# Computing an SSM convolution kernel only at its 641 distinct bf16 positions, and expanding it by DMA

## The chip, the cores and the metric

One core of a Trainium2 chip. The metric is the device time of one execution in microseconds (us), the median of several runs; "span" is the profiled time of the core from its first to its last instruction, about 2 us less. PE is TensorE, DVE VectorE, ACT ScalarE, POOL GpSimd; SP (SyncE) mainly issues DMAs. A run counts as slow when it is over 1.5% above the fastest of its kernel.

## The reference, cut to what matters

```python
def _B_ref(u, A_re, A_im, B_re, B_im, C_re, C_im, log_dt, Dskip):   # u: (1, 2048, 512); A, B, C: (512, 128)
    dt = jnp.exp(log_dt)[:, None]
    logdA = dt * (A_re + 1j * A_im)
    dB = dt * Bc
    l = jnp.arange(L).astype(A_re.dtype)          # bf16: 2048 positions, 641 distinct values
    P = jnp.exp(logdA[:, :, None] * l)            # (512, 128, 2048)
    K = jnp.einsum("dn,dnl,dn->dl", Cc, P, dB).real
    ...                                           # y = irfft(rfft(u) * rfft(K)) + u * Dskip
x = A_x
x = x + attention(layernorm(x)); x = x + _B_ref(layernorm(x))    # and both once more, same weights
```

The positions are rounded to bf16, so above 256 they come in steps of 2, 4 and 8, and several of the 2048 positions share one value of K. K does not depend on x; it is computed once, transformed (the "spectrum"), and used in both convolution layers.

## The kernel before

K at position i·32 + j is the sum over the 128 states of G[i]·Z[j]: two tables of complex powers, 64 by 33, built by repeated doubling on VectorE and contracted on TensorE, for nine chunks of channels. Every doubling is one complex multiply:

```python
def cmul(nc, pool, shape, xr, xi, c, s, out_r, out_i, nz, tag):
    # ... t1, t2 from a pool with one buffer each
    nc.vector.tensor_tensor(t1[:], xr, c, ALU.mult)
    nc.vector.tensor_tensor(t2[:], xi, s, ALU.mult)
    nc.vector.tensor_tensor(out_r, t1[:], t2[:], ALU.add if nz else ALU.subtract)
    # ... t3, t4: the same two buffers again
    nc.vector.tensor_tensor(t3[:], xi, c, ALU.mult)
    nc.vector.tensor_tensor(t4[:], xr, s, ALU.mult)
    nc.vector.tensor_tensor(out_i, t3[:], t4[:], ALU.subtract if nz else ALU.add)
```

The result, `kg_sb`, lies on 64 partitions in 33 KB each. The spectrum relays it to 128 partitions with two DMAs, permutes it into `k_perm` with two copies, and makes the rounding by 20 patch copies (15 on VectorE, 5 on ScalarE).

```python
with tc.tile_pool(name="kpool", bufs=1) as kpool:
    kg_sb = kpool.tile([NI, NJ, D], BF16, name="kg_sb")       # 33 KB, kept until the spectrum is done
    ...
    k_spectrum(tc, nc, kg_sb, C, w2_dram, kf_dram)            # k_perm, then a1s (two buffers), kf_sb (three)
x_sb = xpool.tile([P, NA, D], F32, name="x_sb")               # 32 KB
with tc.tile_pool(name="xin", bufs=1) as tmp:
    xin = tmp.tile([P, NA, D], BF16, name="xin")              # 16 KB
    nc.sync.dma_start(xin[:], A_x...)
    # ... ScalarE: casts into x_sb and the layer-norm sums of its 16 rows
```

The order of instructions on each engine and the addresses of pools are decided by the framework: a scheduler orders, and a pool that is released gives its address to the next one.

## Time and profile before

| | us |
|---|---|
| median of the three runs at the start | 806.27 (802.87 to 843.03; the run of 843.03 was slow) |
| span of the profiled run | 804.0 |
| powers and tables (DVE full) | up to 229 |
| PE tail, relay, copies and patches | 229 to 264.1 |
| spectrum, x's casts and statistics | 264.1 to 326.1 |
| four layers | 326.1 to 804.0 |

The page cuts the span into 40 slices, a digit being the busy share in tenths. Two of its rows, kernel before:

```profile
DVE  7999998989742730358999968665457999968665
DMA  2010000000028263000300027633000300044732
```

This fence shows what an average hides: DVE is full in the first eleven slices (20 us each), then little used for five, then works in the layers. The prediction below shows the same stretches in microseconds.

### The profile page before, as it was taken

To read this page: it belongs to the slowest core of one execution; us is meant where nothing else is said; L and a number is where in the kernel's file an instruction comes from. 1 tells how busy PE (TensorE), PEld (TensorE's weight loads), DVE (VectorE), ACT (ScalarE), POOL (GpSimd) and SP (SyncE) were. 2 spreads that over 40 slices of the span, in tenths; PEclk is the share of its full clock that TensorE was granted. 3 is DMA by queue.
4 is the path that set the end of the run, shared out by engine and by line. 5 is a ranking of instruction groups with operands and counts; after the bars stand their busy time and mean duration, and the time that the engine had idled before them with its cause. 6 is when DMAs were issued, how large, how long until landed. Compare 5 with 4: busy or idle time off the path is not lost. (4 is left out here: it accounts for less than half of the span.)

```text
span 804.0 us, 14299 instructions
## 1 busy us (share of the span) xinstructions
PE 489.9 (61%) x5960; PEld 389.3 (48%) x5960; DVE 601.4 (75%) x1079; ACT 366.0 (46%) x596; POOL 14.6 (2%) x20
## 2 busy tenths in 40 slices
PE   1002877676930720499887767563599887858554
PEld 1002877676930720344655646553344655637553
DVE  7999998989742730358999968665457999968665
ACT  7960223232333669643242337536543243237524
POOL 0000000000000000100000010000100000010000
PEclk9999999999999955599898888787698998887878
DMA  2010000000028263000300027633000300044732
GB/s 46 26 52 0 1 28 27 26 27 27 2 42 278 99 228 94 0 1 2 92 2 1 2 104 233 191 106 104 2 1 1 93 2 2 1 179 155 200 101 104
DMA packets 23318, 53.87 MB, mean 67 GB/s; under 512 B 6203, under 2 KB 8408, under 8 KB 21208
## 3 DMA queue, kind: packets, MB, share of 16 engines
q1 hardware_dynamic: 20870, 49.23, 19.3%
q10 hardware_dynamic: 2304, 2.62, 0.9%
q0 software_dynamic: 80, 1.11, 0.5%
q8 instruction: 46, 0.75, 0.4%
q14 instruction: 18, 0.15, 0.1%
HBM read 36.57 MB, written 10.49 MB: 59 GB/s over the span
## 5 line engine op out<-in xcount | busy, mean ns | idle before, releaser
L813 PE MATMUL pk<-Zr,Gr 128*64 128x33 bf16 x512 | 118.5, 290 | 79.5 <-DVE Gr L672 78.8
L813 PEld LDWEIGHTS <-Gr 128*64 128x64 bf16 x512 | 107.0, 211 | 79.7 <-issue 63.1
L814 PE MATMUL pk<-Zn,Gi 128*64 128x33 bf16 x512 | 117.4, 287 | 25.8 <-DVE Gi L677 25.8
L814 PEld LDWEIGHTS <-Gi 128*64 128x64 bf16 x512 | 105.2, 207 | 27.6 <-DVE Gi L677 27.3
L263 PE MATMUL po<-ident,pav 128*128 128x128 bf16 x1024 | 75.2, 245 | 9.5 <-DVE pav L259 9.2
L263 PEld LDWEIGHTS <-pav 128*128 128x128 bf16 x1024 | 71.7, 113 | 12.5 <-DVE pav L259 12.3
L816 ACT CAST kg_sb<-pk 64x264 bf16<-64x264 f32 x64 | 23.8, 373 | 116.8 <-PE pk L814 116.8
L208 DVE TENSOR_TENSOR prod<-qT,kT_ext 128x2048 bf16<-128x2048 bf16 x64 | 75.1, 1215 | 1.6 <-ACT qT L187 1.6
L259 DVE TENSOR_TENSOR pav<-attn,v_ext 128x2048 bf16<-128x2048 bf16 x64 | 74.4, 1220 | 2.3 <-PE po L263 2.1
L547 PE MATMUL pb<-Wp,t 128*128 128x128 bf16 x256 | 37.7, 241 | 32.9 <-DVE t L535 29.4
L152 PE MATMUL pt<-ident,xn 128*128 128x128 bf16 x128 | 15.8, 278 | 55.9 <-ACT xn L124 54.1
L270 ACT CAST oT<-po 128x1024 bf16<-128x1024 f32 x8 | 8.1, 1012 | 85.2 <-PE po L263 85.2
L211 PEld LDWEIGHTS <-prod 128*128 128x128 bf16 x1024 | 31.1, 97 | 23.6 <-DVE prod L208 16.4
L547 PEld LDWEIGHTS <-t 128*128 128x128 bf16 x256 | 27.7, 109 | 30.2 <-DVE t L535 30.0
L211 PE MATMUL L<-ind,prod 128*128 128x8 bf16 x1024 | 33.8, 167 | 13.0 <-DVE prod L208 13.0
L152 PEld LDWEIGHTS <-xn 128*128 128x128 bf16 x128 | 11.4, 126 | 61.7 <-ACT xn L124 58.1
L534 ACT CAST ub<-pb 128x1024 bf16<-128x1024 f32 x32 | 32.3, 1031 | 19.7 <-DVE t L536 18.4
L500 PE MATMUL pb<-a1s,w_sb 128*128 128x64 bf16 x768 | 32.0, 201 | 15.1 <-DVE kf_sb L479 8.7
L500 PEld LDWEIGHTS <-w_sb 128*128 128x128 bf16 x768 | 28.6, 103 | 17.9 <-issue 15.1
L103 ACT ACTIVATE ln_junk<-x_sb 128x512 bf16<-128x512 f32 x48 | 30.2, 628 | 14.5 <-DVE x_sb L99 13.1
L548 PE MATMUL pb<-WpJ,t 128*128 128x128 bf16 x256 | 36.2, 240 | 0.1
L289 PE MATMUL pq<-wvp,xnT 128*128 128x512 bf16 x128 | 34.7, 414 | 1.0 <-DVE v_ext L294 1.0
(234 smaller groups left out, 1148.9 us busy)
## 6 DMA issues: line engine op xcount, KB each, us to landing
w_sb<-w_dram SPq DMA_DIRECT2D x12, 1024.0 KB, 9.1
kr_c<-kf_dram SPq DMA_DIRECT2D x64, 128.0 KB, 2.9
ki_c<-kf_dram SPq DMA_DIRECT2D x64, 128.0 KB, 2.9
kf_dram<-kf_sb SPq DMA_DIRECT2D x16, 256.0 KB, 3.0
v_ext<-v_ext SPq DMA_DIRECT2D x2, 1568.0 KB, 9.0
w_dram<-w_full SPq DMA_DIRECT2D x4, 512.0 KB, 2.6
w_dram<-w_full ACTq DMA_DIRECT2D x4, 512.0 KB, 2.6
xin<-in_A_x_dram SPq DMA_DIRECT2D x1, 2048.0 KB
```

Source lines behind the costliest of these rows:

```text
L103: nc.scalar.activation(lnst["junk"][:], x_sb[:, a, :], ACT.Square, accum_out=lnst["s2"][:, a:a + 1])
L208: eng.tensor_tensor(pr[:], qT[:, ft].unsqueeze(1).to_broadcast([P, NW, 4, P]), kap, ALU.mult)
L211: nc.tensor.matmul(L[:, al, w0 + wi, ft * 8:(ft + 1) * 8], lhsT=pr[:, wi, al, :], rhs=ind8[:], start=False, stop=True, skip_group_check=True)
L259: eng.tensor_tensor(pv[:], attn[:, :, w, :].unsqueeze(2).to_broadcast([P, 4, DH, H]), v[:, s0:s0 + 4, :].rearrange("p a (d h) -> p a d h", ...
L263: nc.tensor.matmul(po[:, al, ftp, :], lhsT=pv[:, al].rearrange("p d h -> p (d h)")[:, ftp * P:(ftp + 1) * P], rhs=ident[:], start=False, s ...
L289: nc.tensor.matmul(pp[:], lhsT=xnT[:, dt, a * P:(a + 1) * P], rhs=wv[:, dt].rearrange("p d h -> p (d h)"), start=(dt == 0), stop=(dt == ND ...
L500: nc.tensor.matmul(p2[:, j, :], lhsT=self.w2[:, ec * EC + j, :], rhs=a1s[:, ec * EC + j, :], start=True, stop=True)
L534: nc.scalar.copy(ub[:], p2[:].rearrange("p e q -> p q e"))
L547: nc.tensor.matmul(p3[:, j, :], lhsT=t1[:, dql, :], rhs=wp_r, start=True, stop=False)
L548: nc.tensor.matmul(p3[:, j, :], lhsT=t2[:, dql, :], rhs=wpj_r, start=False, stop=True)
L813: nc.tensor.matmul(pk[:, j, :], lhsT=Gr[:, :, dl], rhs=Zr[:, :, dl], start=True, stop=False)
L814: nc.tensor.matmul(pk[:, j, :], lhsT=Gi[:, :, dl], rhs=Zn[:, :, dl], start=False, stop=True)
```

## The change

Intent: compute K at the 641 distinct positions only. They form a rectangle of two tables, 32 powers (multiples of 8, table A) by 21 others (table B); for four groups of channels side by side that fills TensorE's 128 rows. The compact kernel goes to DRAM in 24 stores, and 18 loads expand it to the 2048 positions, repeating rows, so that the patches vanish.

```diff
-        chunks = [(c * DC, DC) for c in range(D // DC - 1)] + [(D - DC, DC // 2), (D - DC // 2, DC // 2)]
-        for dc, (d_lo, dcs) in enumerate(chunks):
-            ...            # two levels of table Z, three of table G, per chunk of 64 channels
+        for c in range(P // CH):                      # 4 chunks of 32 x 4 channels
+            Ar = tb.tile([P, CH, NIA, 4], BF16, name="A_r")
+            ...
+            for k in range(5):
+                J = 1 << k
+                shape = [P, CH, J, 4]
+                y = [t[:, k, qs, :].unsqueeze(2).to_broadcast(shape) for t in (Pr, Pi)]
+                cmul(nc, tmpp, shape, [t[:, :, 0:J, :] for t in (Ar, Ai)], y, [t[:, :, J:2 * J, :] for t in (Ar, Ai)])
+            for q8 in range(CH // 8):
+                ...        # 16 matmuls of 84 columns, one eviction into kgs
+        for g in range(4):
+            ...            # six pieces each
+            for dst, sr in pieces:
+                nc.sync.dma_start(dst, sr)            # 24 stores kgs -> kd_dram, 641 x 512
@@ k_spectrum
-            for jhi in range(2):
-                (nc.sync if jhi == 0 else nc.gpsimd).dma_start(kr0[jhi::2, :, :], kg_sb[:, 16 * jhi:16 * jhi + 17, :])
+            nc.sync.dma_start(dsk[:], ins["Dskip"].partition_broadcast(1))
+            k_load(tc, nc, kr, kd)                    # 18 loads kd_dram -> k_rl, 12 of them with repeated rows
+            nc.vector.tensor_tensor(kr[0:1, 0, :], kr[0:1, 0, :], dsk[:], ALU.add)
             ...            # the two permuting copies stay
-            for (p0, p1, runs) in round_patches():
-                ...        # 20 patch copies and the copy of the first 16 rows
@@ main
-    with tc.tile_pool(name="kpool", bufs=1) as kpool:
-        kg_sb = kpool.tile([NI, NJ, D], BF16, name="kg_sb")
+    kd = dram.tile([NROW, D], BF16, name="kd_dram")
```

## The prediction

> **What bounds the kernel now.** I read the busy tenths of the page first, then the busy time by stretches, then the timelines of VectorE (DVE) and of the DMA-issuing SyncE queue around the ends of those stretches. The page's slices show a first third unlike the rest: DVE full, TensorE (PE) clock full, hardly any DMA. Cut at the events of the timeline, the stretches are (us, then busy us and instruction counts by engine, clock, DMA share, GB/s):
>
> ```profile
> 0.00:15.30 15.30, 3.33 (x24) 2.23 (x24) 11.44 (x47) 11.02 (x23) 1.58 (x13) 1.00 0.26 61
> 15.30:54.70 39.40, 0.00 (x0) 0.00 (x0) 39.12 (x63) 36.03 (x71) 0.00 (x0) 1.00 0.07 27
> 54.70:229.00 174.30, 113.91 (x963) 112.14 (x963) 162.78 (x341) 51.90 (x106) 0.00 (x0) 1.00 0.05 19
> 229.00:236.90 7.90, 6.95 (x62) 6.83 (x62) 0.41 (x1) 1.84 (x5) 0.00 (x0) 1.00 0.00 0
> 236.90:253.20 16.30, 0.00 (x0) 0.00 (x0) 0.00 (x0) 0.02 (x1) 0.69 (x1) 1.00 0.94 251
> 253.20:264.10 10.90, 0.00 (x1) 0.03 (x1) 8.44 (x17) 8.62 (x6) 0.00 (x0) 1.00 0.51 213
> 264.10:326.00 61.90, 20.99 (x512) 19.30 (x512) 19.39 (x20) 49.14 (x85) 0.34 (x1) 0.67 0.42 137
> 326.00:804.00 478.00, 344.74 (x4400) 248.78 (x4400) 359.85 (x592) 207.45 (x305) 11.98 (x5) 0.84 0.23 70
> ```
>
> The columns after the length are PE, weight loads, DVE, ScalarE (ACT), POOL. Up to 54.7 the powers are squared and the first tables built, DVE full. From 54.7 to 229 nine chunks expand both tables by complex multiplies and contract them: DVE 93% busy, PE 114 us hidden under it. From 229 PE finishes alone, from 236.9 everyone waits for the DMA that relays the kernel onto 128 partitions, from 253.2 copies permute and patch it. At 264.1 the spectrum starts. So this whole front is serial and DVE sets 213.7 us of it (15.3 to 229). The rest of the program, 539.9 us, is not touched by the change.
>
> DVE timeline near the end of the tables, and the copies after the relay:
>
> ```profile
> 223.04 0.42 DVE L676 TENSOR_TENSOR c_b<-Gr,pow_i_hi 128x512 bf16<-128x512 bf16 x1
> 223.38 0.68 DVE L670 TENSOR_TENSOR c_a<-Gr,pow_r_hi 128x1024 bf16<-128x1024 bf16 x1
> 223.98 0.42 DVE L677 TENSOR_TENSOR Gi<-c_a,c_b 128x512 bf16<-128x512 bf16 x1
> 224.31 0.69 DVE L436 TENSOR_SCALAR g_i<-g_i 128x1024 int32<-128x1024 int32 x1
> 224.91 0.68 DVE L671 TENSOR_TENSOR c_b<-Gi,pow_i_hi 128x1024 bf16<-128x1024 bf16 x1
> 225.63 0.69 DVE L672 TENSOR_TENSOR Gr<-c_a,c_b 128x1024 bf16<-128x1024 bf16 x1
> 226.36 0.69 DVE L675 TENSOR_TENSOR c_a<-Gi,pow_r_hi 128x1024 bf16<-128x1024 bf16 x1
> 226.97 0.69 DVE L676 TENSOR_TENSOR c_b<-Gr,pow_i_hi 128x1024 bf16<-128x1024 bf16 x1
> ...
> 253.29 1.49 DVE L608 COPY k_perm<-k_rl 128x4096 bf16<-128x4096 bf16 x1 [16.49 <-DMA k_rl<-kg_sb]
> 256.83 1.76 DVE L619 COPY k_perm<-k_perm 32x512 bf16<-32x512 bf16 x7 [2.06 <-ACT k_perm L608]
> 258.62 2.36 DVE L622 COPY k_perm<-k_rl 16x8192 bf16<-16x8192 bf16 x1
> ```
>
> Two things to see. Start to start, a 512-element multiply takes 0.34 us, a 1024-element one 0.60 (and a 2048-element one 1.13, from 172.59 to 173.72): 0.067 us plus 1 us per 1920 elements. And where an operation needs the result just before it (224.91 to 225.63), or overwrites what that one reads (225.63 to 226.36), the step is 0.72 to 0.73, not 0.60: a dependence costs 0.12 us. The old order mostly has another instruction in between.
>
> **What the skill says.** "VectorE: DVE Perf Modes", "The perf-mode tier table": bf16 tensor_tensor from SBUF reaches 2x, 2048 elements in 1224 ns; the trace has 1216 to 1220. "Vector Engine (DVE) Microarchitecture Reference", "5.1 Performance modes": this mode asks for 2-byte types, innermost step of one and more than one element innermost, not for long rows. That matters, as the new tables have innermost runs of 4. No two-source instruction here has such short rows, but the 16x8192 copy into runs of 4 took 2.36 us, far above one element per cycle. "DMA: Bandwidth & Descriptors", "Anatomy of one DMA": a fixed cost near 2 us, mostly the write receipt; here the stores of the spectrum landed in 2.0 us at the least and 2.9 in the median. Its "Specifications" want 512 B for line rate and say that smaller transfers are read-modify-written; the new scatter writes 256 B rows, and no row of this trace is a store of that kind.
>
> **The change part by part.** The 2048 positions rounded to bf16 have 641 distinct values, in place of 64x33 computed ones.
>
> *Setup.* Twelve powers for eleven, so 11 squarings. The 21-entry table B takes 7 complex multiplies over 13 blocks of 512: 13x512 = 6,656 elements, times 6 instructions, the same 6,656 as the old first tables. 6x6,656/1920 = 20.8 us, plus 42x0.067 = 2.8: 23.6 us. Little is saved here.
>
> *Chunks.* Before, each of 512 channels got 80 new table entries: 80x512x6 = 245,760 elements, plus table copies. Now table A gets 31 entries in 4 chunks of 32x4 channels: 3,968x6x4 = 95,232 elements in 120 instructions: 49.6+8.0 = 57.6 us, against 174.3 wall.
>
> *DVE sum from 15.3* (where the first power is ready in both): squarings 20x0.60 = 12.0; B 23.6; A 57.6; the rest of the C.B product 2.4; sine constants and small ones, now all inside this phase, 10.6: 106.2 us. The built order of instructions runs each complex multiply as two products, a sum that needs them, and so on, in the same pair of temporaries: 4 dependences in 6. 20x4 for A and about half that rate for B, less the interleaved constants, gives some 85x0.12 = 10 us. The middle squarings have no table work beside them and are paced by ACT (four instructions of 0.52 us start to start per level): 4 us idle. Tables end at 15.3+106.2+10+4 = 136 (estimate), against 229.
>
> *PE.* 256 matmuls of 84 columns for 1,024 of 33 at 0.117 us each. They hide except in the last chunk: 64 matmuls; the first matmul pairs of the spectrum, 128 columns, were 0.105 us apart at half clock, so I take 0.085: 5.4 us, plus the last eviction (264 columns took 0.37, 1024 took 1.01, so about 0.7 for 672). End 142; this tail was 7.9 and is 6.
>
> *Relay.* Removed: the two DMAs (16.3 us, slowed by the 4 MB of the DFT table beside them) and 10.9 us of copies with patches. Added, all on the SyncE queue: 24 stores of the compact kernel to DRAM, then 18 loads with broadcast rows. They are issued one at a time, each also waiting for the eighth one before it. Issues here took 0.32 (128 rows), 0.59 (64 rows), 0.59 to 0.69 (32 rows), 0.84 to 0.90 us (odd shapes); I take 0.55. Ahead of them in the queue are the skip vector and a quarter of the DFT table: 1.5 us. So 1.5 + 24x0.55 (13.2) + landing 2.5 + 18x0.55 (9.9) + landing 2.6 = 29.7. Then the skip add 0.4 and the two permuting copies (ACT's took 3.6): 4.1. Spectrum start 142+29.7+4.1 = 176.
>
> *Sum.* 264.1-176 = 88 us: 93 from the tables, 2 from the tail, 7 given back (34 us of relay for 27). 804-88 = 716 us. What follows is taken as unchanged: the remaining 3 MB of the DFT table are issued behind the loads but needed only some 7 us after the spectrum starts.
>
> **The rivals.** (1) Runs of 4 lose the 2x mode. Then A costs 95,232/960+8 = 107 us and B 44: 70 us more, about 786. For: no two-source proof in the trace. Against: the rule looks at the innermost step alone, and the copies with the same runs kept their fast mode. About 6%. (2) DMA takes the place of DVE: 256 B stores or the chain of 42 issues cost twice what I take. Issues of 0.9 us would add 15 us, slow stores some 15 more: 730 to 745. For: every odd-shaped DMA here cost 0.8 to 0.9. Against: the 256 B loads at the start (512 rows each) landed in 2.3 to 3.8 us with issues of 0.37 to 0.50. (3) ACT becomes the bound, having all sine constants and 44 power copies in less time: its work from 47 to 76 is about 28 us, so it fits under DVE, but a late constant stalls DVE in order; up to 8 us. (4) Issues as cheap as 0.35 and no idle in setup: some 12 us better, 704.
>
> **Range and chances.** These sum to more room upwards than downwards: 716, range 700 to 742. A gain under 2% would need 788 us or more: mode loss together with a slow relay. The fast runs before were 802.9 and 806.3, so their spread hardly matters. Faster 0.97, within 2% 0.02, slower 0.01.
>
> **What would show it.** The 128x2048 multiply of table A at 1.22 us (2.29 would be rival 1); DVE over 90% busy from 15 to about 136; dependent steps 0.12 us longer; table phase 57.6 plus some 9 us for four chunks; PE under 2 us busy per group of 16 matmuls; stores and loads on the SyncE queue together near 30 us, and their single issue times; copies after it, then the spectrum start at about 176; from there to the end 540 us. The prediction is wrong if the relay runs past 45 us, if DVE shows idle time waiting for ACT constants over 10 us, or if the part after the spectrum start changes by more than 5 us, say because the late DFT table holds up its second stage.

## The result and the profile after

| | before | after |
|---|---|---|
| median of four runs, us | 804.57 (801.53 to 843.03) | 717.88 (716.43 to 718.44) |
| span of the profiled run | 804.0 | 715.9 |

The ratio is 0.892 (95% interval 0.888 to 0.896): 11% less time. A ratio is the mean time of one kernel's fast runs over that of the other's of the same rounds, so it is not quite the ratio of the medians. Predicted were 716 us, 700 to 742.

The same two rows of the page, kernel after (a slice is now 18 us):

```profile
DVE  7999999304500348899995867635689999858665
DMA  2002110237661000300002766040003000083622
```

DVE's full stretch is 7 slices instead of 11, and the gap behind it did not shrink. By stretches, kernel after (start:end, length, then busy us and instruction counts of PE, weight loads, DVE, ACT, POOL; PE's clock, DMA share, GB/s):

```profile
15.00:61.57 46.57, 0.00 (x0) 0.00 (x0) 45.88 (x86) 44.27 (x85) 0.00 (x0) 1.00 0.06 23
61.57:131.50 69.93, 12.95 (x194) 11.84 (x194) 67.21 (x130) 32.56 (x54) 0.00 (x0) 0.73 0.11 46
131.50:136.80 5.30, 3.85 (x62) 3.69 (x62) 0.51 (x1) 2.84 (x4) 0.00 (x0) 0.69 0.00 0
136.80:167.50 30.70, 0.00 (x0) 0.00 (x0) 0.41 (x1) 0.00 (x0) 0.00 (x0) 0.52 0.59 142
...
168.90:236.20 67.30, 19.69 (x512) 17.82 (x512) 18.91 (x17) 51.51 (x85) 0.35 (x1) 0.65 0.44 155
236.20:715.90 479.70, 341.71 (x4374) 251.15 (x4400) 359.63 (x596) 208.06 (x306) 11.96 (x5) 0.83 0.23 70
```

Both table stretches keep DVE over 96% busy, so DVE still sets their end. In the relay's 30.7 us no compute engine works. The stage from the spectrum start to the end of the statistics is 67.8 us (168.9 to 236.8; the stretch above is cut 0.6 us too early); its counterpart before was 62.0.

DVE's timeline at the end of the last table, kernel after:

```profile
127.13 1.23 DVE L629 TENSOR_TENSOR A_r<-cm_a,cm_b 128x2048 bf16<-128x2048 bf16 x1
128.39 1.22 DVE L631 TENSOR_TENSOR cm_a<-A_i,pow_r 128x2048 bf16<-128x2048 bf16 x1
129.53 1.22 DVE L632 TENSOR_TENSOR cm_b<-A_r,pow_i 128x2048 bf16<-128x2048 bf16 x1
130.78 1.22 DVE L633 TENSOR_TENSOR A_i<-cm_a,cm_b 128x2048 bf16<-128x2048 bf16 x1
```

1.22 us for 2048 elements although the innermost run is 4: the fast mode held. Start to start, the independent pair (128.39, 129.53) is 1.14 us apart, the dependent pair (129.53, 130.78) 1.25. The DMA issues of SyncE, kernel after (start, length, instruction, count):

```profile
136.80 14.83 SPq L780 DMA_DIRECT2D kd_dram<-kgs  x24
...
152.15 9.04 SPq L803 DMA_DIRECT2D k_rl<-kd_dram  x17
161.23 1.73 SPq L458 DMA_DIRECT2D w_sb<-w_dram  x3
178.38 14.70 SPq L599 DMA_DIRECT2D kf_dram<-kf_sb  x12
193.81 0.33 SPq L861 DMA_DIRECT2D xin<-in_A_x_dram  x1
```

and the last two kinds in the kernel before:

```profile
273.54 3.71 SPq L635 DMA_DIRECT2D kf_dram<-kf_sb  x4
277.42 0.33 SPq L876 DMA_DIRECT2D xin<-in_A_x_dram  x1
```

The relay takes 14.8 us of stores and 9.5 us of loads (the first of the 18 is not in the row above), near what was worked out, and then 6.3 us until the last load has landed. But look at the load of x: before, it was issued behind 4 stores of the spectrum, 13.3 us after the spectrum start (264.1); after, behind 12 of them, 24.9 us after its start (168.9). ACT's casts and statistics of x, some 31 us in series, wait for it and end the stage. That is the 6 us, and the question of the experiments is what delays x.

### The profile page after: what moved, and what is told of

Read it like the earlier page. It is cut to its first block, busy times and chain, and to the rows that moved or that the text cites. A ratio compares the mean times of both kernels' runs of the same rounds, so it can differ in the third digit from the quotient of the medians.

```text
span 715.9 us, 12534 instructions
## 1 busy us (share of the span) xinstructions
PE 381.7 (53%) x5166; PEld 286.6 (40%) x5192; DVE 504.4 (70%) x873; ACT 351.0 (49%) x552; POOL 13.8 (2%) x19
## 5 line engine op out<-in xcount | busy, mean ns | idle before, releaser
L259 PE MATMUL po<-ident,pav 128*128 128x128 bf16 x1024 | 77.4, 250 | 9.0 <-DVE pav L255 8.9
L259 PEld LDWEIGHTS <-pav 128*128 128x128 bf16 x1024 | 74.4, 115 | 11.6 <-DVE pav L255 11.4
L760 PE MATMUL pk<-B_r,A_r 128*128 128x84 bf16 x128 | 16.5, 251 | 95.6 <-DVE A_r L629 95.6
L760 PEld LDWEIGHTS <-A_r 128*128 128x128 bf16 x128 | 15.0, 130 | 96.2 <-ACT w_qi L398 66.8
L207 PE MATMUL L<-ind,prod 128*128 128x8 bf16 x1024 | 33.8, 167 | 13.2 <-DVE prod L204 13.1
L496 PE MATMUL pb<-a1s,w_sb 128*128 128x64 bf16 x768 | 31.0, 197 | 9.0 <-DVE kf_sb L475 3.3
L285 PE MATMUL pq<-wvp,xnT 128*128 128x512 bf16 x122 | 32.0, 391 | 2.0 <-DVE v_ext L290 1.5
L486 PE MATMUL pb<-F1c,u 128*64 128x128 bf16 x256 | 21.0, 251 | 21.6 <-issue 21.3
L275 PE MATMUL pq<-wop,oT 128*128 128x512 bf16 x120 | 28.9, 379 | 6.7 <-ACT oT L266 6.1
L473 ACT CAST z<-pb 128x1024 bf16<-128x1024 f32 x16 | 16.2, 1012 | 32.7 <-PE pb L544 32.5
L496 PEld LDWEIGHTS <-w_sb 128*128 128x128 bf16 x768 | 27.4, 100 | 12.1 <-issue 9.2
```

Source lines behind the costliest of these rows:

```text
L207: nc.tensor.matmul(L[:, al, w0 + wi, ft * 8:(ft + 1) * 8], lhsT=pr[:, wi, al, :], rhs=ind8[:], start=False, stop=True, skip_group_check=True)
L259: nc.tensor.matmul(po[:, al, ftp, :], lhsT=pv[:, al].rearrange("p d h -> p (d h)")[:, ftp * P:(ftp + 1) * P], rhs=ident[:], start=False, s ...
L275: nc.tensor.matmul(pw[:], lhsT=oT[:, al, ftp, :], rhs=wo[:, ftp, :], start=(ftp == 0), stop=(ftp == NDT - 1))
L285: nc.tensor.matmul(pp[:], lhsT=xnT[:, dt, a * P:(a + 1) * P], rhs=wv[:, dt].rearrange("p d h -> p (d h)"), start=(dt == 0), stop=(dt == ND ...
L496: nc.tensor.matmul(p2[:, j, :], lhsT=self.w2[:, ec * EC + j, :], rhs=a1s[:, ec * EC + j, :], start=True, stop=True)
L760: nc.tensor.matmul(o, lhsT=ta[:, ql].rearrange("p i g -> p (i g)"), rhs=tbb[:, c * CH + ql].rearrange("p b g -> p (b g)"), start=(kx == 0) ...
```

## The experiments

All outputs are right. Each edit is against the changed kernel unless it says otherwise; ratios are to the kernel before, where the change alone has 0.892. One hundredth of ratio is 8 us. The medians are over all timed executions; those of pad (one of 2002 us) and best_c (one of 678.79) include one slow execution, which the ratios leave out.

| run | median us | ratio | 95% |
|---|---|---|---|
| xin_pool | 724.28 | 0.898 | 0.895 to 0.901 |
| before_xin_pool | 809.77 | 1.005 | 1.001 to 1.009 |
| cmul_order | 708.26 | 0.878 | 0.875 to 0.881 |
| two_queues | 712.85 | 0.885 | 0.882 to 0.889 |
| pad | 715.35 | 0.886 | 0.883 to 0.889 |
| pad2 (same program) | 710.62 | 0.883 | 0.881 to 0.886 |
| before_pad | 811.81 | 1.007 | 1.004 to 1.009 |
| w2_early | 719.32 | 0.892 | 0.889 to 0.894 |
| x_early | 693.66 | 0.861 | 0.858 to 0.864 |
| big_first | 722.78 | 0.899 | 0.895 to 0.902 |
| best_b | 675.73 | 0.841 | 0.838 to 0.844 |
| best_c | 675.38 | 0.837 | 0.832 to 0.841 |

### What delays x: first theory, the queue (xin_pool, before_xin_pool)

```diff
-        nc.sync.dma_start(xin[:], A_x.rearrange("b (p a) d -> p (b a) d", p=P))
+        nc.gpsimd.dma_start(xin[:], A_x.rearrange("b (p a) d -> p (b a) d", p=P))
```

> The changed kernel with one word different: the load of x is issued by GpSimd's queue, not by SyncE's, where it stood behind 12 spectrum stores (before the change: behind 4). My theory of the 7.1 us that the part after the spectrum start lost: x is issued 24.9 us after that start instead of 13.3, and ScalarE's 31 us of casts and statistics, which end the stage, follow it. Then x is issued about 13 us after the start, the statistics end 59 to 62 us after it instead of 67.3, and the whole is 6 us shorter (3 to 10): ratio to the kernel before about 0.884 where the change alone had 0.892. The rival, that the late quarters of the DFT table or slow spectrum stores stretch the stage: x arrives sooner but the evictions and stores still end late, and the total stays within 2 us.

> The kernel before the change with the load of x on GpSimd's queue. There x was issued 13.3 us after the spectrum start, as soon as its buffer was free, so my theory expects little: within 2 us of the kernel before (0 to -2), and the part from the spectrum start to the end as long as in the changed kernel with the same edit, to 2 us. If instead both kernels gain alike, the queue's order is not what made the parts differ, and the 7 us have another cause (the clock, the late table).

The first miss: the changed kernel became 5 to 6 us slower, not faster. On its new queue, with nothing ahead of it, x was issued at 196.69, 26.9 us after the spectrum start. What POOL waited for, run xin_pool (engine, instruction, releaser: us, times, longest):

```profile
POOL xin L861 <- DVE kf_sb L475: 193.7, 1, 193.7
```

It waited for an eviction of the spectrum's second stage, which has nothing to do with x's data. That pointed to a wait for the buffer. So the twelve stores ahead of x in SyncE's queue were a symptom: the scheduler put x where its buffer comes free. (POOL's load landed 9.9 us after its issue.) The kernel before lost 3 to 4 us with the same edit (809.77 against 806.49), where at most a gain of 2 was expected; its issue, 14.2 us after the spectrum start, was hardly later than before. The second half of that expectation missed too: from the spectrum start to the end the two kernels with the same edit took 542.1 and 552.4 us, so they still differ by 10 us, and the queue is not what makes them differ.

### Second theory, the address (pad, pad2, before_pad)

The compiled programs' buffer maps (byte of the partition where each starts) say:

```
                     before             after
kg_sb   (33 KB)      29600              -
k_perm  (16 KB)      63392              29600
a1s, 1st and 2nd     79776, 96160       45984, 62368
x_sb    (32 KB)      29600              29600
xin     (16 KB)      62368              62368
```

Before, xin lay on the end of kg_sb and on k_perm, which is free when the first stage has read it. With kg_sb gone everything slid down, and xin lies exactly on the second a1s buffer, read until the last matmuls of the second stage. What SyncE waited for before it issued x's load (L861), run after:

```profile
SPq L861 <- PE pb L496: 0.6, 1, 0.6
```

L496 is the second stage's matmul: its last one ends at 193.78, and x is issued at 193.81. In the kernel before, x is issued at 277.42, 0.4 us after the last matmul that reads k_perm (277.05). If this is the cause, 33 KB of padding undo it, and padding in the kernel before brings it in:

```diff
+    padp = tc.alloc_tile_pool(name="padp", bufs=1)                # pad: where kpool was
+    padt = padp.tile([P, 33, D], BF16, name="padt")
+    nc.vector.memset(padt[:, 0, 0:1], 0.0)
     btmp = tc.alloc_tile_pool(name="ctmp_b", bufs=1)
     ...
     k_spectrum(tc, nc, kd, ins, C, w2_dram, kf_dram)
+    padp.release()
```

```diff
     with tc.tile_pool(name="xin", bufs=1) as tmp:                 # before_pad: in the kernel before
+        padt = tmp.tile([P, 33, D], BF16, name="padt")
+        nc.vector.memset(padt[:, 0, 0:1], 0.0)
         xin = tmp.tile([P, NA, D], BF16, name="xin")              # now at 96160, the second a1s
```

> The changed kernel with a 33 KB buffer, touched once and otherwise unused, where the kernel before kept its kernel table until the spectrum was done. New theory of the 7 us that the later part lost, after the queue swap made nothing faster: the change took that 33 KB buffer away, so the buffers above slid down, and x's landing buffer now lies at the address of the second first-stage buffer of the spectrum, which is read until the spectrum's last matmuls, where before it lay on the permuted kernel, free after the first stage. So x can't be fetched earlier, whatever queue issues it. With the pad the addresses are those of before: x is issued 13 to 15 us after the spectrum start, not 24.9, the statistics end 60 to 63 us after it, not 67.3, total 6 us less (3 to 9). Rival (the late quarters of the DFT table, or spectrum stores): within 2 us of the changed kernel.

> The reverse in the kernel before: its buffer for x alone is pushed up by 33 KB (an unused tile ahead of it in the same pool), onto the second first-stage buffer of the spectrum, as in the changed kernel. Theory of the addresses: x is issued some 25 us after the spectrum start instead of 13.3, the statistics end 65 to 69 us after it instead of 61.4, and the total is 6 us longer than the kernel before (3 to 9; ratio 1.004 to 1.011). Rival (what the change itself did to the table or the stores): no difference, ratio 0.998 to 1.002.

> The same program as the one labelled pad, run again because its only profiled execution took 2002 us (every engine several times slower than elsewhere) and shows no usable durations; its five timed ones gave 0.8862 of the kernel before. Theory of the addresses: in a normal profile x is issued behind 4 stores, 13 to 16 us after the spectrum start instead of 24.9, the statistics end 61 to 64 us after it instead of 67.3, total 711 to 716. If the statistics still end 67 us after it, the gain came from elsewhere and the theory falls.

The one profiled execution of pad took 2002 us, for no reason that I can name; its durations are not used. SyncE's issues in before_pad, then in pad2:

```profile
274.43 15.48 SPq L635 DMA_DIRECT2D kf_dram<-kf_sb  x12
290.74 0.33 SPq L878 DMA_DIRECT2D xin<-in_A_x_dram  x1
```

```profile
178.94 3.71 SPq L599 DMA_DIRECT2D kf_dram<-kf_sb  x4
182.77 0.36 SPq L865 DMA_DIRECT2D xin<-in_A_x_dram  x1
```

and pad2 by stretches from its spectrum start:

```profile
169.47:230.90 61.43, 21.06 (x512) 19.42 (x512) 18.91 (x17) 50.64 (x85) 0.35 (x1) 0.64 0.51 171
230.90:710.20 479.30, 344.82 (x4400) 247.80 (x4400) 360.11 (x596) 208.03 (x306) 11.95 (x5) 0.83 0.23 70
```

| | x issued after the spectrum start | statistics end after it | spectrum start to end |
|---|---|---|---|
| before | 13.3 | 62.0 | 539.9 |
| before_pad | 26.3 | 70.1 | 548.9 |
| after | 24.9 | 67.8 | 547.0 |
| pad2 | 13.3 | 62.1 | 540.7 |

The address alone moves the stage both ways, by 6 to 8 us and the whole later part by 6 to 9, and with the old addresses the later part of the changed kernel is as long as that of the kernel before, to 1 us. These are single profiled executions (before_pad's was its slowest); by the medians the totals move by 6 us (before_pad) and 7 us (pad2). The 4 and 12 stores ahead of x come and go with it, and x follows the last reader of its bytes each time: in before_pad the last second-stage matmul ends at 290.71 and x is issued at 290.74, in pad2 the last matmul on k_perm ends at 182.45 and x is issued at 182.77. This settles the cause. It also answers the prediction's own guess:

### The late DFT table (w2_early)

```diff
+    cb["w2"] = ...   # a buffer at the far end of memory; its four loads after chunk 3, not at the spectrum
```

> The changed kernel with the 4 MB DFT table fetched in four pieces during the last chunk of table A, into its own buffer at the far end of memory, where the DMA engines are idle, instead of around the relay. Theory: the last three quarters saturated the DMA engines beside the last loads of the relay (6.1 us to land, where a lone one took 2.1), and the first quarter took the queue's time ahead of the stores: the spectrum starts 3 us sooner (2 to 5), and that reaches the end: total 3 us less (1 to 5). Rival: the late table also held the part after the spectrum start; then the statistics end less than 65 us after that start and the total falls by 6 or more. Other rival: the loads land no sooner, the total stays within 1 us.

Neither the theory nor the first rival: ratio 0.892 as without the edit, the spectrum start at 169.29, the rest 548.1. The other rival is right, the loads land no sooner. The 6.1 us that the largest load takes do not come from the table (5.9 us with it away), and the late table did not hold the end. It did slow the first stores: beside its first quarter, issued just ahead, the first store landed 4.9 us after its issue, with the table away 2.0.

### Dependences (cmul_order)

```diff
-    t1, t2 = tmp("cm_a"), tmp("cm_b")
+    t1, t2, t3, t4 = tmp("cm_a"), tmp("cm_b"), tmp("cm_c"), tmp("cm_d")
     nc.vector.tensor_tensor(t1, xr, yr, ALU.mult)
     nc.vector.tensor_tensor(t2, xi, yi, ALU.mult)
-    nc.vector.tensor_tensor(out[0], t1, t2, ALU.subtract)
-    t3, t4 = tmp("cm_a"), tmp("cm_b")
     nc.vector.tensor_tensor(t3, xi, yr, ALU.mult)
     nc.vector.tensor_tensor(t4, xr, yi, ALU.mult)
+    nc.vector.tensor_tensor(out[0], t1, t2, ALU.subtract)
     nc.vector.tensor_tensor(out[1], t3, t4, ALU.add)
```

> The changed kernel with each complex multiply as four products into four temporaries, then the difference and the sum: the same six instructions, but only one in six now follows its own input directly. Theory (VectorE sets the end of the tables, and a dependence on the neighbour costs 0.12 us): some 70 to 85 dependences at 0.12 us, so the tables end 8 to 10 us sooner, at 122 to 124 instead of 132.0, and all of it reaches the end: 8 us (6 to 10) off the total. Rival (TensorE or ScalarE paces the chunks, or the dependence costs nothing): tables within 2 us of 132, total within 2 us.

DVE's timeline at the end of the last table, run cmul_order:

```profile
118.34 1.22 DVE L630 TENSOR_TENSOR cm_d<-A_r,pow_i 128x2048 bf16<-128x2048 bf16 x1
119.47 1.22 DVE L631 TENSOR_TENSOR A_r<-cm_a,cm_b 128x2048 bf16<-128x2048 bf16 x1
120.61 1.22 DVE L632 TENSOR_TENSOR A_i<-cm_c,cm_d 128x2048 bf16<-128x2048 bf16 x1
```

Same instructions, same 1.22 us each, but 1.13 to 1.14 us start to start, also between the last product and the difference that it does not feed. The tables end at 121.8 instead of 132.0, 10.2 us sooner, and the total falls by about as much (9.6 by the medians). Counted in the trace, 74 of the 161 steps that follow an instruction of these multiplies in the changed kernel come 0.11 to 0.19 us later than the prediction's formula for independent ones (0.067 us plus 1 us per 1920 elements), 9.3 us in all; in cmul_order none of 162 does. Theory confirmed: DVE sets that end. The prediction's 85 dependences of 0.12 us were some 10 too many, and their sum of 10 us was the right size.

### What bounds the relay (two_queues, big_first)

```diff
-                nc.sync.dma_start(dst, sr)
+                (nc.sync if n % 2 == 0 else nc.scalar).dma_start(dst, sr)     # and so for 17 loads
```

> The changed kernel with its 24 stores and 17 expanding loads of the relay issued in turn by SyncE's and ScalarE's queues instead of SyncE's alone. Theory (the relay is bound by issuing one after the other, 24 x 0.618 and 18 x 0.525 us): 14.8 us of stores become about 8 and 9.5 us of loads about 5, while landings and the table's DMA stay: relay 31.4 to 19 us (17 to 22), total 10 to 13 us less. Rival (the DMA engines are bound by the many short rows, or eight outstanding per queue holds them): the relay keeps over 28 us and the total moves by at most 3.

A miss: spectrum start at 164.6 instead of 168.9, 4 us and not 10 to 13. ACT issued its 12 stores in 8.65 us, SyncE needed 12.91 for its 12. What SyncE's queue waited for, run two_queues, and the stretch of the loads:

```profile
SPq L780 <- DMA kd_dram<-kgs: 5.0, 3, 4.6
SPq L803 <- DMA k_rl<-kd_dram: 4.5, 4, 3.0
```

```profile
149.80:163.00 13.20, 0.00 (x0) 0.00 (x0) 0.41 (x1) 0.03 (x1) 0.00 (x0) 0.50 0.99 181
```

With one queue the waits were 0.3 (stores, for a load of the table) and 1.0 (loads). The program lets a DMA start only when an earlier one, eight places back, has landed; issuing faster runs into that. And in the loads' stretch the DMA engines were 99% busy at 181 GB/s, moving rows of 1 KB. (The last 4 us of that stretch hold the table's loads too; from 154 to 159, before they are issued, it was 188 to 214 GB/s. The busy share counts overlapping packets and passes 1 in such short slices.) So the stores were bound by issuing, as expected (24 of 0.618), but just behind that bound stand the landings, and the loads are nearly bound by the engines themselves. SyncE's one long wait, 4.6 us, was for a store that landed beside the table's first quarter; two queues with the table away were not run together. The Trainium skill ("DMA: Bandwidth & Descriptors", "Issuing engines are not separate DMA queues") says that all issuers share the same DMA engines and that a second issuer saves only sequencer time; this run agrees, with 4 us.

The next edit takes the loads largest first instead of smallest first:

```diff
-    for o, (p0, p1, base) in enumerate(((16, 32, 256), (32, 64, 384), (64, 128, 512))):
+    for o, (p0, p1, base) in ((2, (64, 128, 512)), (1, (32, 64, 384)), (0, (16, 32, 256))):
-        for (t, a0, cnt) in runs:
+        for (t, a0, cnt) in sorted(runs, key=lambda r: -r[2]):
         # and the plain load of the first 16 rows moves from first to last
```

> The changed kernel with the relay's loads ordered from the largest (448 KB, 64 rows times 7 copies) to the smallest, instead of ending with the largest. Before this I held the loads to be bound by issuing (0.525 us each); the run without the table beside them landed no sooner and showed the DMA engines 80 to 99% busy at some 200 GB/s in the last 6 us, in 1 KB rows. If the end is the drain of the large loads, starting them first overlaps it with the issues of the small ones: the last load lands 2 to 4 us sooner and the total falls by 2 to 4 us (ratio 0.887 to 0.890). If issuing is the bound, or the bytes are the bound from the first load on, the total stays within 1 us.

Another miss, 5 us slower. SyncE's waits, run big_first:

```profile
SPq L802 <- DMA k_rl<-kd_dram: 4.3, 6, 1.3
```

Small loads now waited for large ones to give back their place (4.3 us, against 1.0), so the issues ended 3 us later, and the first row, to which the skip vector is added (0.41 us), came last instead of first: spectrum start at 171.28, 2.4 us later (0.8 of it arose before the relay began). The remaining 2 to 3 us of the difference were not traced.

### Using the idle relay (x_early), and the combinations (best_b, best_c)

ACT is idle in the relay and then runs x's casts and statistics in series. x_early gives x a buffer at the far end of memory, fetches it early and puts that work right behind the tables; both permuting copies go to DVE.

```diff
+    cb["xin"] = ...; nc.sync.dma_start(cb["xin"][:], A_x...)          # after the setup of k_gen
     btmp.release()
+    for h in range(4):
+        nc.scalar.copy(x_sb[:, h * 4:(h + 1) * 4, :], cb["xin"][:, h * 4:(h + 1) * 4, :])
+        ln_stats_part(nc, lnst, x_sb, h * 4, h * 4 + 4)
```

> The changed kernel with x fetched at the start of the chunks into a buffer at the far end of memory, its casts and statistics (ScalarE, 31 us) issued right after the tables, while everyone waits for the relay, and both permuting copies on VectorE (1.28 us each). If ScalarE's serial 31 us is what ends the stage after the spectrum start, as my reading of the 7 us says, those 31 us now lie beside the relay, the stage ends with the spectrum's own work some 28 to 40 us after its start instead of 67.3, and the total is 30 us less (25 to 36), about 688. Rival (the stage is set by spectrum stores and buffers, or ScalarE is late for the first evictions): less than 15 us.

Confirmed, at the low edge or just under it: 24 to 25 us less. Three lines of DVE's timeline in x_early tell what was lost:

```profile
19.88 0.68 DVE L688 TENSOR_TENSOR zr<-mag,cs 128x512 f32<-128x512 f32 x1
...
177.00 2.37 DVE L122 TENSOR_SCALAR xn<-x_sb,ln_rstd,ln_nb 128x512 bf16<-128x512 f32 x5
179.28 2.53 DVE L585 COPY k_perm<-k_rl 128x4096 bf16<-128x4096 bf16 x2
```

The first power came at 19.88, not at 14.25: the scheduler moved x's 2 MB to the very start, ahead of the inputs. And the first layer's normalisation went ahead of the permuting copies, so the spectrum started at 180.7. best_b mends both (x's load is made to depend on table B's last entry; x's casts run on DVE, so that the statistics end sooner), and takes the cmul order, large loads first and ten kf_sb buffers instead of three:

```diff
+            after_setup(Bn[:, 0, 19, :]) ... nc.scalar.copy(cb["xin"][:, 0, 0:4], late)   # then x's load
+        fb = FftB(tc, nc, C, w2_dram, kf_dram, ctx, grp_bufs=2, wk_bufs=10)
```

best_c is best_b with the loads smallest first again.

> All that worked, and three mends, in one kernel: complex multiplies as four products, then two sums (9.6 us found); x fetched early, but only after the last entry of table B is written, so that its 2 MB no longer delay the inputs of the first power (5.6 us lost to that in the earlier run); its casts on VectorE, idle in the relay, so that ScalarE's statistics take 24 us and end before the loads; large loads first; ten buffers in place of three for the spectrum's output, whose evictions waited for their stores. Sum from the early-x run's 694: 9.6 + 5.6 for the tables, 6 for the permuting copies that waited there behind the first layer's normalisation, 2 for the loads, 5 to 9 for the output buffers: 664 (655 to 675), ratio 0.824. Rival: the DMA queue, now with the weights, the table and the stores close together, takes the gain of the buffers back: 672 to 680.

> The combined kernel with the relay's loads back in their old order, smallest first; nothing else differs from the combined kernel before it. Large loads first cost the changed kernel 5 us (small loads waited behind large ones for one of eight places, and the first row, which the skip vector is added to, came last), so here the loads should land about 3 us sooner after the end of the tables, the spectrum start at 157 to 159 instead of 161.2, and the total be 5 us less than the combined kernel's: 670 (667 to 673), ratio 0.834. If the gain is less than 2 us, the stretch after the spectrum start does not follow its start but the weights of the first layer.

best_b missed by 12 us, best_c by 5. Both beat the changed kernel by some 6% (best_c 0.837 against 0.892). best_c's spectrum started 1.5 us earlier than best_b's (159.7 against 161.2), not 3; the intervals of the two overlap, so the order of the loads is not told apart here. What the sums lacked is in DVE's waits after the spectrum start, run best_c:

```profile
DVE xnT L149 <- ACT xn L120: 6.2, 1, 6.2
DVE ln_mean L104 <- DMA wop<-in_A_wo_dram: 5.4, 1, 5.4
```

The normalisation, whose first steps ran at the end of the relay in x_early (172.5 to 179), now ran after the spectrum, from 189.4 to 202.3, 12.9 us in series. The view puts the wait of ln_mean down to the weights (wop), which is what best_c's expectation named as its alternative. But ln_mean waits for all eight semaphores of the DMA queue at once, and it starts at 189.42, just after the last of the sixteen kf_sb stores has landed (189.30); the first load of wop lands only at 191.6. In best_b it is the same: 191.64 and 191.76. So it waited for the stores. best_b's rival is not refuted either: its time lies in that rival's 672 to 680, and in best_c, with the weights' loads among them, the stores took 6.4 us to land in the median, against 2.6 in the changed kernel. By the buffer map, ln_mean (156576) lies on one of the ten kf_sb buffers (156576; with three buffers, as in x_early, on none): very likely the same trap again, set by me. Fewer buffers were not run, so this last step is argued and not shown.

## Why the prediction was right

By its own steps, predicted and measured (us):

| step | predicted | measured |
|---|---|---|
| tables end | 136 | 132.0 |
| of it dependences | 10 | 9.3 (74 late steps; 10.2 by cmul_order) |
| of it idle in setup | 4 | under 1 (45.88 busy of 46.57) |
| PE tail | 6 | 4.7 (132.0 to 136.7) |
| relay | 29.7 | 31.4 (136.05 to 167.5) |
| of it ahead of the stores | 1.5 | 0.75 |
| of it 24 stores | 13.2 | 14.8 |
| of it landing of the stores | 2.5 | 0.1 |
| of it 18 loads | 9.9 | 9.5 |
| of it landing of the loads | 2.6 | 6.3 |
| add and copies before the spectrum starts | 4.1 | 1.4 (167.5 to 168.9) |
| spectrum start | 176 | 168.9 |
| from there to the end | 539.9, "unchanged" | 547.0 |
| sum | 716 | 715.9 |

- The mechanism holds for the front: the tables set the end on DVE, the fast mode survived rows of 4, the relay is a chain of issues about as long as worked out. Rivals 1 (mode lost) and 3 (ACT bound) are dead by the 1.22 us and by DVE's 96 to 98% busy; rival 2 (transfers twice as dear) by the 31.4 us; rival 4 (issues at 0.35) by 0.618 and 0.53.
- The closeness of the sum is luck. The front came 7 us earlier than predicted and the rest 7 us later.
- So, in part, is that of the relay. Its two landing terms were taken alike, 2.5 and 2.6 us. The first did not appear: the first load was issued at 151.73, 0.1 us after the issue of the last store; the last store of this load's own rows, issued at 148.05, had landed at 150.0. The second was 6.3, the drain of the largest loads. (The page section that the prediction names for the fixed cost near 2 us describes DMAs issued from GpSimd; these are SyncE's, and only the trace's 2.0 and 2.9 us bear on them.)
- The step that failed is "What follows is taken as unchanged": 7.1 us more, where the prediction's own sign of being wrong was a change over 5. It named the late DFT table; w2_early shows that the table is innocent. The cause is the removed pool: 33 KB gone, buffers moved, xin on the second a1s, x 11.6 us later after the spectrum start. pad2 gets 540.7 for this term, before_pad takes the kernel before to 548.9.
- Of the front's 7 us, 4 come from the tables, mostly the setup idle that did not come (under 1 us for 4: in the DVE timeline constants and the C·B product stand between the squarings, which are 22 instructions and not the 20 of the sum, 1.2 us more), 1.3 from the tail, 2.7 from the copies: the spectrum's first matmuls need only DVE's half of the permutation, 1.28 us, while ACT's 3.6 us run beside them. The relay gave 1.7 back.

## What to carry to other kernels

A change that adds or removes a buffer moves every buffer behind it, and a load can inherit a new wait far from the diff: compare the buffer maps, and when a DMA waits for an instruction that has nothing to do with its data, look whose bytes it will overwrite. On an engine that sets the end, order independent instructions between dependent ones before looking for anything cleverer; here that was about 1.5% for no work saved. And when two errors can cancel, check the steps of a prediction, not its sum.

## What the Trainium skill lacked or had wrong

- "VectorE: DVE Perf Modes", "The DRAIN you can't avoid": it says that the next operation does not start until the pipe empties, adding that one which is not held starts earlier, and that a semaphore costs nothing extra (measured on copies). Here a 2048-element bf16 multiply started 1.13 to 1.14 us after an independent one of 1.22 us, 0.08 us before that one's end, and 1.25 us after one that it depends on. The section gives no price for that dependence: 0.12 us each in most cases, 9.3 us in this kernel.
- "DMA: Bandwidth & Descriptors", "Specifications": transfers under 512 B are said to be read-modify-written. The stores of 256 B rows landed in medians of 1.9 (32 KB) to 3.4 us (64 KB) beside the table's load, and of 1.8 to 1.9 (16 to 64 KB) with it away (w2_early); the spectrum's stores of 256 KB took 2.6 and 2.1 in the same two runs. No price of it stands out at this size, though no run has the same bytes in longer rows. The page gives no bandwidth of this chip for rows of 1 KB: the relay's loads drew 188 to 214 GB/s with the DMA engines full (two_queues, 154 to 159), where the DFT table's loads (8 KB rows) drew 365 to 420 (slices of the changed kernel around 168).
- The same page, "Issuing engines are not separate DMA queues": it calls the time to issue usually small beside the transfer. For many small DMAs it was not: 24 stores took 14.8 us to issue, 0.618 each, and SyncE waited only 0.3 us between them.
- No page was found on what a reused on-chip address does to a load: 11.6 us of delay and 6 to 9 us of the later part, for 33 KB of shift.
